# Threshold attention and a GELU MLP on one core: new sizes for the MLP portions of each slot, the fifth pair of heads turned by VectorE, x^T behind the next scores, and p regrouped in halves

## The chip, the cores and the metric

The kernel runs on one core of one Trainium2 chip. The metric is the time of one execution on the device in microseconds (us). Each kernel is run several times, and every run of the kernel before that is quoted beside it was made on the same chip. Two chips were used: the runs on the tail copies, gelus at once, regrouping whole and the loads were made on one, the other eight runs of the experiments on the other, so a comparison between those two groups, of traces too, crosses chips. A kernel on one core has no second core to compare its clock with, so single runs are compared through medians and 95% intervals.

Engines are named as the profile names them: PE is TensorE (PEld its weight loads), DVE is VectorE, ACT is ScalarE, POOL is GpSimd, SP is SyncE.

## The reference

Attention for 8 batches of 8 heads, 576 rows and 64 columns. In each row only the scores within tau = 0.02 of the row's maximum are kept. The 8 heads of a row, side by side, are the input x of an MLP with an exact GELU. All is float32, but the MLP's weights arrive as float64 and must be converted on the chip.

```python
def _attn_ref(q, k, v, tau):
    scale = 1.0 / np.sqrt(q.shape[-1])
    scores = scale * np.matmul(q, k.transpose(0, 1, 3, 2))
    thresh = np.max(scores, axis=-1, keepdims=True) - tau
    scores = np.where(scores >= thresh, scores, -1000000000.0)
    scores = scores - np.max(scores, axis=-1, keepdims=True)
    attn = np.exp(scores)
    attn = attn / (np.sum(attn, axis=-1, keepdims=True) + 1e-09)
    return np.matmul(attn, v).astype(np.float32)

def _moe_ref(x, w_in, w_out):          # x: 4608 x 512, w_in: 512 x 2048
    h = x @ w_in
    g = 0.5 * h * (1.0 + erf(h / sqrt(2)))
    return (g @ w_out).astype(np.float32)
```

## The kernel before

Two heads make a pair; there are 32 pairs of 5 chunks (four of 128 query rows and a tail of 64 rows of each head), hence 160 **slots**. In each slot PE makes the scores of one chunk, DVE takes the row maximum, ACT the exp, DVE masks and sums (this frees the score banks in PSUM), then p is transposed ("turned"), and the MLP of tokens that are ready fills PE's spare time. The first 20 slots take chunks 0 and 1 of the first four pairs, then their other chunks.

There are two ways of turning. For *early* pairs PE transposes q, k and p by products with the identity or with a diagonal that also scales. For *late* pairs DVE transposes blocks of 32 x 32 into `pd`, and DMA regroups those into `pT`. Then x^T = v^T p^T is a product on PE.

```python
    EARLY = HP + 1                  # HP = 4: five pairs are turned by PE

    def turn_p(p, i):               # a late pair, chunk i, by VectorE
        ...
        for e in reversed(range(n)):
            to = pd_tail[p % 2] if i == NC else pd[e][:, :, i * Q:(i + 1) * Q]
            nc.vector.transpose(to[:, 0:NB, :], w[:, e * S:(e + 1) * S].rearrange("p (b i) -> p b i", i=Q))
        if i == NC - 1:             # all four main chunks are there: regroup them in eight transfers
            s["pT"] = [one.tile([P, KR, S], FP32, tag=f"pT{e}", name=f"pT{e}") for e in range(2)]
            for e in range(2):
                for a in range(4):
                    regroup(s["pT"][e], a * P, P, pd[e], a)
        ...
    def block_steps(n):             # the MLP of one block of 256 tokens
        ...                         # hT: 4 products with w_in for each j
            if j % 2:
                t = gp.tile([P, 2, TOK], FP32, tag="g", name="g")
                nc.scalar.activation(t, hT, AF.Gelu)
        ...                         # o_ps: products with w_out

    PART = (1.0, 1.2, 1.0, 1.0, 0.8)          # share of MLP work in each slot of a pair
    for n in range(len(slots) + WEIGH + 1):   # [cut] the loop over slots
        scores(p, i)
        softmax_head(p, i)                    # maximum, exp
        owed += (goal(n) - goal(n - 1)) * BLK_NS * (PART[i] if not early and p < NP else 1.0)
        if early and n % 2:
            fill(owed, tokens)                # MLP, in every other early slot
        if last and last[0] < EARLY:
            turn_p_early(*last)               # PE turns the slot before
        softmax_tail(p, i, early)             # mask, sum, scale
        if not early and i:
            for c in range(0 if i == 1 else i, i + 1):
                turn_p(p, c)
        ...
        convert(3000 if n < 2 * HP else 3400) # float64 weights to float32, on VectorE
        ...                                   # x^T of early pairs
        if not early:
            fill(owed, tokens)
        if p > EARLY and i == WEIGH:          # x^T of the pair before, at the end of its slot
            for h in range(2):
                weigh_v(p - 1, h * HALF, (h + 1) * HALF)
```

## Time and profile before

| | before |
|---|---|
| median of 3 runs | 1493.13 us (1492.93 to 1494.76) |
| the profiled run | 1498.07 us, span 1496.3 us |
| granted PE clock, mean | 0.988 |
| PE / DVE / ACT busy | 97% / 61% / 43% of the span |

### The profile page before, as it was taken

What the parts mean: (1) busy time and instruction counts of PE and PEld (TensorE: products, weight loads), DVE (VectorE), ACT (ScalarE), POOL (GpSimd) and SP (SyncE); (2) the same over time, 40 slices, a digit from 0 to 9 for tenths busy, and PEclk for the clock granted to TensorE, in tenths of its full rate; (3) what the DMA queues carried; (4) which work ended last, traced back from release to release, by engine and by line L of the source; (5) the groups of instructions that cost most, each with busy time, mean ns of one, the idle gap of its engine ahead of it and who ended that gap; (6) DMA issues with size and microseconds to landing.
All of it is one profiled execution on the core that took longest, in us unless ns stands there. A gap on an engine that the chain in (4) does not pass through costs nothing.

```text
span 1496.3 us, 17938 instructions
## 1 busy us (share of the span) xinstructions
PE 1451.5 (97%) x6388; PEld 921.7 (62%) x6388; DVE 908.4 (61%) x2083; ACT 644.2 (43%) x952; POOL 40.5 (3%) x86
## 2 busy tenths in 40 slices
PE   7889898999999999999999999999999999999998
PEld 5567565547475756565666656565656575765764
DVE  6887748787767777777767766776676676000000
ACT  5566545736464545444444435363535252110110
POOL 3122000000000000000000000000000000000000
PEclk9899999999999999999999999999999999999999
DMA  9867313556555555554545455555554433200000
GB/s 281 251 217 237 80 32 80 112 118 120 107 109 104 107 107 102 104 104 96 104 83 106 97 117 104 117 103 111 98 109 94 98 73 70 57 15 11 4 14 14
DMA packets 381448, 152.12 MB, mean 102 GB/s; under 512 B 225456, under 2 KB 370608, under 8 KB 381360
## 3 DMA queue, kind: packets, MB, share of 16 engines
q1 hardware_dynamic: 371792, 116.84, 39.0%
q0 software_dynamic: 7168, 33.54, 6.6%
q8 instruction: 52, 0.85, 0.2%
q10 hardware_dynamic: 2400, 0.59, 0.2%
q14 instruction: 36, 0.29, 0.1%
HBM read 61.85 MB, written 9.44 MB: 48 GB/s over the span
## 4 chain that ended last, share of the span: by engine, by line
PE 87%; DVE 6%; DMA 3%; ACT 2%; SPq 2%; issue 1%; DVEq 0%; ACTq 0%
PE o_ps L454 32%; PE hT L443 32%; PE sc L339 11%; PE xT L415 10%; DVE p L364 2%; SPq L404 2%; DVE nmx L350 2%; PE tr L285 1%; DVE pd L392 1%; DMA q<-in_q_dram 1%; DMA k<-in_k_dram 1%; ACT p L351 0%; DMA pT<-pd 0%; ACT L351 0%; DVE power L176 0%
## 5 line engine op out<-in xcount | busy, mean ns | idle before, releaser
L443 PE MATMUL hT<-x,w_in 128*128 128x256 f32 x2304 | 524.2, 385 | 0.0
L454 PE MATMUL o_ps<-w_out,g 128*128 128x512 f32 x1152 | 515.4, 598 | 0.0
L443 PEld LDWEIGHTS hT<-x,w_in 128*128 128x128 f32 x2304 | 437.1, 192 | 88.3 <-issue 28.1
L454 PEld LDWEIGHTS o_ps<-w_out,g 128*128 128x128 f32 x1152 | 214.8, 190 | 259.3 <-issue 256.1
L350 DVE TENSOR_REDUCE nmx<-sc 128x1 f32<-128x576 f32 x288 | 205.7, 751 | 250.1 <-PE sc L339 249.8
L351 ACT ACTIVATE p<-sc,nmx 128x576 f32<-128x576 f32 x288 | 202.5, 740 | 302.5 <-DVE nmx L350 302.1
L364 DVE SCALAR_TENSOR_TENSOR p<-sc,thr,p 128x576 f32<-128x576 f32 x288 | 225.3, 816 | 56.8 <-ACT p L351 44.8
L415 PE MATMUL xT<-pT,v 128*64 128x288 f32 (+2 forms) x1280 | 171.0, 418 | 11.1 <-issue 4.7
L339 PE MATMUL sc<-kT,qT 64*128 64x288 f32 x960 | 160.0, 437 | 9.5 <-DVE p L364 9.1
L392 DVE STREAM_TRANSPOSE pd<-p 128x576 f32<-128x576 f32 x216 | 151.7, 750 | 5.8 <-DMA pT<-pd 5.2
L415 PEld LDWEIGHTS xT<-pT,v 128*64 128x64 f32 x1280 | 93.7, 140 | 85.6 <-issue 20.9
L339 PEld LDWEIGHTS sc<-kT,qT 64*128 64x128 f32 x960 | 88.6, 189 | 84.7 <-issue 65.0
L447 ACT ACTIVATE g<-hT 128x512 f32<-128x512 f32 x144 | 85.3, 597 | 124.7 <-PE hT L443 123.8
L380 DVE TENSOR_SCALAR p<-p,rden 128x576 f32<-128x576 f32 x215 | 104.6, 518 | 4.7
L351 ACT ACT_TABLE_LOAD x78 | 100.1, 1283 | 13.4 <-DVE nmx L350 12.2
L447 ACT ACT_TABLE_LOAD x79 | 101.4, 1283 | 9.4 <-PE hT L443 8.0
L424 ACT COPY x<-xT 128x256 f32<-128x256 f32 (+7 forms) x124 | 28.8, 285 | 145.9 <-PE xT L415 145.9
L457 ACT COPY o_sb<-o_ps 128x512 f32<-128x512 f32 x36 | 21.0, 583 | 150.2 <-PE o_ps L454 147.0
L285 PE MATMUL tr<-diag,p 128*128 128x128 f32 (+1 forms) x450 | 57.2, 290 | 0.0
L285 PEld LDWEIGHTS tr<-diag,p 128*128 128x128 f32 (+1 forms) x450 | 50.2, 187 | 11.2 <-issue 4.1
L378 ACT ACTIVATE p<-p,rden 128x576 f32<-128x576 f32 x28 | 21.7, 776 | 42.7 <-DVE rden L369 42.7
L339 PE MATMUL sc<-kT,q_tail 128*128 128x288 f32 x120 | 34.5, 410 | 5.5 <-DVE p L364 5.4
(69 smaller groups left out, 466.8 us busy)
## 6 DMA issues: line engine op xcount, KB each, us to landing
pT<-pd SPq DMA_DIRECT2D x216, 320.0 KB, 5.9
out_dram<-o_sb SPq DMA_DIRECT2D x36, 256.0 KB, 2.4
pT<-pd_tail SPq DMA_DIRECT2D x108, 80.0 KB, 3.2
q<-in_q_dram SPq DMA_DIRECT2D x108, 72.0 KB, 2.6
k<-in_k_dram SPq DMA_DIRECT2D x108, 72.0 KB, 2.9
v<-in_v_dram SPq DMA_DIRECT2D x162, 40.0 KB, 2.2
raw<-in_moe_w_in_dram POOLq DMA_DIRECT2D x8, 512.0 KB, 8.5
pd<-in_moe_w_in_dram POOLq DMA_DIRECT2D x8, 512.0 KB, 5.9
```

The costliest lines, as they stand in the source:

```text
L285: nc.tensor.matmul(to, lhsT=w[:, cols], rhs=diag[:, e, :], start=True, stop=True)
L339: nc.tensor.matmul(sc[e][:, h, 0:HALF], lhsT=lhsT, rhs=s["kT"][rows, at:at + HALF], start=True, stop=True)
L350: nc.vector.tensor_reduce(nmx[:, e:e + 1], sc, axis=AXIS.XY, op=ALU.max, negate=True)
L351: nc.scalar.activation(w[:, e * S:(e + 1) * S].rearrange("p (h s) -> p h s", h=2), sc, AF.Exp, bias=nmx[:, e:e + 1], scale=1.0)
L364: nc.vector.scalar_tensor_tensor(row, sc[e][:, :, 0:HALF], thr[:, e:e + 1], row, op0=ALU.is_ge, op1=ALU.mult, accum_out=den[:, e:e + 1])
L380: nc.vector.tensor_scalar(row, row, rden[:, e:e + 1], None, op0=ALU.mult)
L392: nc.vector.transpose(to[:, 0:NB, :], w[:, e * S:(e + 1) * S].rearrange("p (b i) -> p b i", i=Q))
L404: nc.sync.dma_start(to[:, :, at:at + n], src[a * Q:(a + 1) * Q])
L415: nc.tensor.matmul(xT[f, 0:hi - lo], lhsT=s["v"][:, e, c, :], rhs=pT[:, c, lo:hi], start=(c == 0), stop=(c == KR - 1))
L443: nc.tensor.matmul(hT[:, j % 2, :], lhsT=w_in_sb[c][:, j * P:(j + 1) * P], rhs=x_blk[n][:, c, :], start=(c == 0), stop=(c == N_DM - 1))
L447: nc.scalar.activation(t, hT, AF.Gelu)
L454: nc.tensor.matmul(o[:, 0:d_model], lhsT=g[j][:, m * P:(m + 1) * P], rhs=w_out_sb[j], start=(j == 0), stop=(j == N_DF - 1))
```

## The change

It has these parts. (1) MLP portions of late slots are fitted to each slot's room up to slot 42, and are nearly even from there. (2) The fifth pair is turned by VectorE, no longer by PE. (3) x^T stands directly behind the next scores instead of at a slot's end. (4) p is turned in every slot and regrouped in two halves, so that the transfers start earlier. (5) Gelus are held back by up to two, so that the next slot's exps go first, and a small exp brings its table back ahead of need. (6) Early slots have an MLP portion each, and the tail chunk's transposes come after the mask. (7) Some copies of the q and k tails go from VectorE to ScalarE, and some of the scalings of p in the other direction. (8) Later loads of q, k and v are issued from GpSimd.

```diff
-    EARLY = HP + 1
+    EARLY = HP
@@ load(p)
+        eng = nc.sync if p < HP + 2 else nc.gpsimd
-                    nc.sync.dma_start(t[e * D + f:e * D + f + Q], rows[:, :, f:f + Q])
+                    eng.dma_start(t[e * D + f:e * D + f + Q], rows[:, :, f:f + Q])
@@ turn_qk_early: tails of q and k
-        nc.vector.tensor_copy(kT[:, S:S + TAIL], tr[:, 1, 0:TAIL])
+        nc.scalar.copy(kT[:, S:S + TAIL], tr[:, 1, 0:TAIL])
[two more of this kind cut]
@@ softmax_tail
-            if e == 0 and n == 2 and p < 3 * HP:
+            if e == 0 and n == 2 and shared:      # ScalarE scales
@@ regroup(p, i), called at i = 2 (as 1), 3 and 4
+            half = slice((i - 1) * Q, (i + 1) * Q)
+            for e in (1, 0):
+                nc.sync.dma_start(s["pT"][e][:, :, a * P:(a + 1) * P][:, :, half], pd[e][rows, :, half])
@@ the MLP
+    def gelus(left):
+        while len(late) > left:
+            g, j, hT = late.pop(0)
+            ...
+            nc.scalar.activation(t, hT, AF.Gelu)
+    def table():                                  # a tiny exp brings the exp table back
+        if dirty[0]:
+            nc.scalar.activation(warm[:, 1:2], warm[:, 0:1], AF.Exp)
-                nc.scalar.activation(t, hT, AF.Gelu)
+                late.append((g, j, hT))
+                gelus(lag[0])
@@ the loop over slots
-    PART = (1.0, 1.2, 1.0, 1.0, 0.8)
+    PARTS = (1.36, 1.36, 0.5, 1.36, 0.42), (1.1, 1.1, 0.5, 1.2, 1.1)
+        if not early or n % 2 == 0:
+            gelus(0)
+            table()
+        for args in due:                          # x^T of early pairs, one slot later
+            weigh_v(*args)
+        if p > EARLY and i == WEIGH:              # x^T of late pairs, behind the scores
+            for h in range(2):
+                weigh_v(p - 1, h * HALF, (h + 1) * HALF)
-        if early and n % 2:
+        if early:
             fill(owed, tokens)
-        if last and last[0] < EARLY:
+        if last and last[0] < EARLY and last[1] < NC:
             turn_p_early(*last)
-            softmax_tail(p, i, early)
-            if not early and i:
-                for c in range(0 if i == 1 else i, i + 1):
-                    turn_p(p, c)
+            softmax_tail(p, i, early, batch == 1 and not busy)
+            if not early:
+                turn_p(p, i)
+                if i == 2:
+                    regroup(p, 1)
+                if i > 2:
+                    regroup(p, i)
+        if last and last[0] < EARLY and last[1] == NC:
+            turn_p_early(*last)
+            lag[0] = 2 if p < NP else 0
[cut: the last weight pieces leave pd; loads of the fifth pair; when tokens become ready]
```

More of the change, by code (lines that the diff above doesn't have):

```diff
@@ L138, in load_piece @@
         k = loaded[0] - 1
-        if k % 2:
+        if k % 2 and k < len(pieces) - 4:
             room = pd[k // 2 % 2][:, 0:NB - 2, :].bitcast(U32).rearrange("p b i -> p (b i)")
@@ L216, in load @@
                 n = min(KR, NB - r * KR)
-                nc.sync.dma_start(t[r:P:4, e, 0:n, :], rows[:, r * KR:r * KR + n, :])
+                eng.dma_start(t[r:P:4, e, 0:n, :], rows[:, r * KR:r * KR + n, :])
     def load_early(p):
@@ L267, in turn_qk_early @@
             nc.tensor.transpose(tr[:, j, 0:TAIL], s.pop(name)[0:TAIL, NC, :], ident[0:TAIL, 0:TAIL])
-        nc.vector.tensor_copy(kT[:, S:S + TAIL], tr[:, 1, 0:TAIL])
-        nc.vector.tensor_copy(kT[D:P, 0:TAIL], tr[D:P, 1, 0:TAIL])
+        nc.scalar.copy(kT[:, S:S + TAIL], tr[:, 1, 0:TAIL])
+        nc.scalar.copy(kT[D:P, 0:TAIL], tr[D:P, 1, 0:TAIL])
         for e in range(2):
             rows = slice(e * D, (e + 1) * D)
-            nc.vector.tensor_scalar(
-                qt[rows, e * TAIL:(e + 1) * TAIL], tr[rows, 0, 0:TAIL], q_scale[rows], None, op0=ALU.mult)
+            nc.scalar.activation(
+                qt[rows, e * TAIL:(e + 1) * TAIL], tr[rows, 0, 0:TAIL], AF.Copy, bias=0.0, scale=q_scale[rows])
     def turn_p_early(p, i):
@@ L354, in softmax_head, with softmax_tail @@
         nc.vector.tensor_scalar(thr[:, 0:n], nmx[:, 0:n], -1.0, tau_eff, op0=ALU.mult, op1=ALU.subtract)
-    def softmax_tail(p, i, early):
+    def softmax_tail(p, i, early, shared):
         s = st[p]
@@ L392, in turn_p, with regroup @@
             nc.vector.transpose(to[:, 0:NB, :], w[:, e * S:(e + 1) * S].rearrange("p (b i) -> p b i", i=Q))
-        if i == NC - 1:
+    def regroup(p, i):
+        s = st[p]
+        if i == 1:
             s["pT"] = [one.tile([P, KR, S], FP32, tag=f"pT{e}", name=f"pT{e}") for e in range(2)]
-            for e in range(2):
-                for a in range(4):
-                    regroup(s["pT"][e], a * P, P, pd[e], a)
-        if i == NC:
-            for a in range(4):
-                e, at = divmod(a * Q, TAIL)
-                regroup(s["pT"][e], MAIN + at, Q, pd_tail[p % 2], a)
-    def regroup(to, at, n, src, a):
-        nc.sync.dma_start(to[:, :, at:at + n], src[a * Q:(a + 1) * Q])
+        for a in range(4):
+            rows = slice(a * Q, (a + 1) * Q)
+            if i == NC:
+                e, at = divmod(a * Q, TAIL)
+                nc.sync.dma_start(s["pT"][e][:, :, MAIN + at:MAIN + at + Q], pd_tail[p % 2][rows])
+                continue
+            half = slice((i - 1) * Q, (i + 1) * Q)
+            for e in (1, 0):
+                nc.sync.dma_start(s["pT"][e][:, :, a * P:(a + 1) * P][:, :, half], pd[e][rows, :, half])
     def weigh_v(p, lo, hi):
@@ L431 @@
     BLK_NS = N_DF * (N_DM * NS_IN + TOK // P * NS_OUT)
+    late = []
+    lag = [1]
+    dirty = [False]
+    warm = const.tile([P, 2], FP32, name="warm")
+    nc.vector.memset(warm, 0.0)
+    def gelus(left):
+        while len(late) > left:
+            g, j, hT = late.pop(0)
+            t = gp.tile([P, 2, TOK], FP32, tag="g", name="g")
+            nc.scalar.activation(t, hT, AF.Gelu)
+            g[j - 1], g[j] = t[:, 0, :], t[:, 1, :]
+            dirty[0] = True
+    def table():
+        if dirty[0]:
+            nc.scalar.activation(warm[:, 1:2], warm[:, 0:1], AF.Exp)
+            dirty[0] = False
     def block_steps(n):
-        g = []
+        g = {}
         for j in range(N_DF):
@@ L445, in block_steps @@
             if j % 2:
-                t = gp.tile([P, 2, TOK], FP32, tag="g", name="g")
-                nc.scalar.activation(t, hT, AF.Gelu)
-                g += [t[:, 0, :], t[:, 1, :]]
+                late.append((g, j, hT))
+                gelus(lag[0])
         for m in range(TOK // P):
@@ L451, in block_steps @@
                 yield NS_OUT, len(pieces) - N_DF + j + 1
+                if j not in g:
+                    gelus(0)
                 if j == 0:
@@ L495 @@
     WEIGH = 2
-    START = 2 * HP + 1
+    START = 2 * HP + 2
     GOAL = [(-1, 0.0), (START - 1, 0.0), (BATCH - 1, 0.55)]
@@ L505, in goal @@
         return GOAL[-1][1]
-    PART = (1.0, 1.2, 1.0, 1.0, 0.8)
+    PARTS = (1.36, 1.36, 0.5, 1.36, 0.42), (1.1, 1.1, 0.5, 1.2, 1.1)
     tokens = 0
     owed = 0.0
+    due = []
     for n in range(len(slots) + WEIGH + 1):
@@ L519 @@
             softmax_head(p, i)
-        owed += (goal(n) - goal(n - 1)) * BLK_NS * (PART[i] if not early and p < NP else 1.0)
-        if early and n % 2:
+        busy = len(late)
+        if not early or n % 2 == 0:
+            gelus(0)
+            table()
+        for args in due:
+            weigh_v(*args)
+        due = []
+        if p > EARLY and i == WEIGH:
+            for h in range(2):
+                weigh_v(p - 1, h * HALF, (h + 1) * HALF)
+        owed += (goal(n) - goal(n - 1)) * BLK_NS * (PARTS[n > 2 * BATCH + WEIGH][i] if not early and p < NP else 1.0)
+        if early:
             fill(owed, tokens)
             owed = 0.0
-        if last and last[0] < EARLY:
+            table()
+        if last and last[0] < EARLY and last[1] < NC:
             turn_p_early(*last)
         if p < NP:
-            softmax_tail(p, i, early)
-            if not early and i:
-                for c in range(0 if i == 1 else i, i + 1):
-                    turn_p(p, c)
+            softmax_tail(p, i, early, batch == 1 and not busy)
[7 more added lines that the diff above has]
+            turn_p_early(*last)
         if p < HP - 1 and i == 0:
@@ L539 @@
         if p < HP and i == NC and 0 < p < HP - 1:
-            if p + 3 < EARLY:
-                load_early(p + 3)
-                load_v_early(p + 3)
-            else:
-                load(p + 3)
+            load(p + 3)
         if n == BATCH:
@@ L550 @@
         if p >= HP - 1 and i == 2 and p + 1 < NP:
-            (turn_qk if p + 1 >= EARLY else turn_qk_early)(p + 1)
+            turn_qk(p + 1)
         convert(3000 if n < 2 * HP else 3400)
-        if last and last[0] < EARLY:
-            done, hp = divmod(last[0], HP)
-            if last[1] == 1:
-                weigh_v(last[0], 0, TOK)
-                if hp == HP - 1:
-                    tokens = done * S + TOK
-            if last[1] == NC:
-                weigh_v(last[0], TOK, S)
-                if hp == HP - 1:
-                    tokens = (done + 1) * S
         if not early:
+            lag[0] = 2 if p < NP else 0
             fill(owed, tokens)
             owed = 0.0
-        if p > EARLY and i == WEIGH:
-            for h in range(2):
-                weigh_v(p - 1, h * HALF, (h + 1) * HALF)
-            if p % HP == 0:
-                tokens = p // HP * S
-    convert(1e12)
+        if last and last[0] < EARLY:
+            if last[1] == 1:
+                due.append((last[0], 0, TOK))
+            if last[1] == NC:
+                due.append((last[0], TOK, S))
+        if n == START - 1:
+            tokens = TOK
+        elif n == BATCH + 1:
+            tokens = S
+        elif p > EARLY and i == WEIGH and p % HP == 0:
+            tokens = p // HP * S
     fill(1e12, B * S)
```

## The prediction

> **What bounds the kernel now.** I read the page first: TensorE (PE) is busy 97% of a 1496.3 us span, and the chain that ended last is 87% PE. Busy time does not say whether PE runs at its pace, so I then asked for busy time by stretch and for PE's waits. Columns of the first fence: stretch, its length, then busy us (and instructions) of PE, PEld, VectorE (DVE), ScalarE (ACT), POOL, the granted clock, the DMA share, GB/s. In the second: who waited for whom, total us, times, longest, for the first 220 us.
>
> ```profile
> 11.40:88.50 77.10, 63.91 (x393) 45.81 (x393) 67.30 (x163) 46.53 (x93) 15.81 (x29) 0.91 0.83 257
> 88.50:174.40 85.90, 77.32 (x430) 57.56 (x429) 65.33 (x161) 55.70 (x95) 15.10 (x31) 0.94 0.68 206
> 174.40:333.70 159.30, 148.07 (x652) 87.26 (x654) 112.25 (x263) 78.88 (x120) 0.62 (x2) 0.97 0.39 78
> ...
> 400.00:1255.00 855.00, 855.00 (x3754) 530.69 (x3754) 604.97 (x1364) 390.54 (x535) 0.00 (x0) 1.00 0.51 102
> ```
> ```profile
> PE sc L339 <- DVE p L364: 7.7, 8, 2.3
> PE tr L259 <- DMA q<-in_q_dram: 6.5, 1, 6.5
> PE xT L415 <- issue: 4.7, 2, 2.6
> PE xT L415 <- DVE pT L296: 3.6, 4, 2.5
> ```
>
> The reader is to see that from 400 us on PE never stops, at full clock, while DVE has 250 us to spare in 855. Starts of successive hT records there are 216 ns apart, of o_ps records 429 ns, with about 0.09 us more at each change of kind; nothing but PE work can be taken out of that part. All loss that can be recovered lies before about 330 us: PE idles, the clock falls to 0.91, and DVE (67.3 of 77.1 us in the first stretch) is nearly the limit. I count slots (one chunk of scores, softmax and turning) by their score groups (sc, L339): slot 20 starts at 171.3 us, slot 26 at 223.2, slot 42 at 327.1. From slot 42 on the MLP work left is the same in both programs, so **the question is when slot 42 starts**.
>
> Four lines of the merged timeline (start, duration, instruction, idle before) show the costliest habit of the early part:
>
> ```profile
> 97.85 1.42 PE L285 MATMUL tr<-diag,p 128*128 128x128 f32 x10
> 98.94 0.76 DVE L296 COPY pT<-tr 128x256 f32<-128x256 f32 x2 [3.18 <-PE tr L285]
> ...
> 99.51 3.15 PE L415 MATMUL xT<-pT,v 128*64 128x320 f32 x20 [0.25 <-DVE pT L296]
> ...
> 100.08 0.82 DVE L364 SCALAR_TENSOR_TENSOR p<-sc,thr,p 128x576 f32<-128x576 f32 x1
> ```
>
> VectorE stands 3.18 us for a transpose that PE put behind 5.9 us of MLP, and only then masks p, which releases the score banks.
>
> **What the Trainium skill says.** (1) "ScalarE: Activation LUTs", What ACT_TABLE_LOAD costs: 1283 ns for the load and about 1380 ns of drain. The trace agrees on the load (157 of mean 1283 ns) but shows no drain: an exp ends at 96.27, the load starts at 96.29 and the next ACTIVATE at 97.58. (2) "TensorE: Matmul & The Clock Gate", Part 1: after idle windows of 3.4 us the clock is halved. The trace agrees: halved stretches of 3.41 or 6.83 us, eight of them (34.1 us in all) between 24 and 291 us, then none until the last 3 us. (3) "Perfetto Trace Analysis", Summary: the profiler window per engine type: on the software path an issue lasts until its descriptors are written. Before, POOL's issues of 128 rows take 0.533 us, so at most 4.2 ns a row. (4) "SBUF — State Buffer", SBUF: two separate sides: VectorE's two-port operations keep GpSimd from writing descriptors. No run here shows it yet; the change moves 26 pairs of loads there.
>
> **The change part by part.** I compared the two programs' order of instructions, and costed it with durations from the trace.
>
> *Fifth pair by VectorE.* PE loses 55 transposes (3219 matmuls become 3164), of two records at 112 ns: 12.3 us. DVE gains nine transposes of p (0.72 each), five to nine scalings (0.52) and 1.7 for q and k.
>
> *Slots 0 to 9.* The q/k tails (1.05 us of DVE a pair: 0.22 + 0.23 + 0.58) go to ScalarE, with their waits for PE (1.84 and 0.95). DVE is the pace here, three of them fall inside: 3 x 1.05 + about 2 of waits, **-5**.
>
> *Slots 10 to 19.* MLP portions come in each slot (3.0 us) instead of every other (5.6), the tail's transposes come after the mask, and x^T comes behind the next scores. I walked the slots with two rules: scores start when PE is done and the last mask has ended; DVE starts when the scores (1.25 us) and its own work are done. Full slot: 3.75 us to rden, plus 3.55 of weight conversion; tail slots 2.9 + 3.55; slots 11, 14, 17 carry 1.2 of tail copies and about 1.2 of waiting for PE; slot 17 also turns the fifth pair's q and k. In slots 12, 15 and 18 PE has 1.17 scores + 3.2 x^T + 3.0 MLP + 2.25 transposes, and needs banks that ScalarE frees only after two exps, a table load, a gelu, another load and the copies: about 11 to 13 us each. The last weight pieces no longer lie in pd; one takes block 0's x tile and waits for its hT in slot 18: about 3 us. The walk gives 86 us, and before has 85.9: **0**.
>
> *Slots 20 to 25.* Before 174.4 to 224.5 (DVE starts), 50 us. After: the pair as below 31, slot 25 some 6, conversions and tail copies left over 4.5: 41.5, **-8.6**.
>
> *Slots 26 to 41.* The portions 1.36, 1.36, 0.5, 1.36, 0.42 give PE 5.9, 5.9, 7.9, 5.9, 2 us a slot, plus 0.25 for changes of kind. DVE per full slot, from the timeline of slot 28 (reduce at 231.41, rden done 235.16, turned 237.2): 5.75, or 6.3 where it scales both halves; 1.73 more in slot 2, 4.25 in the tail slot. Neither exceeds the other by much; the walk gives 31 us a pair. Before, these 16 slots took 103.9 us (6.5 a slot, with PE waiting 9.6 for masks after 220 us and DVE 12 for exps between 175 and 345, behind table loads); after 16/5 x 31 = 99: **-5**.
>
> *From slot 42.* PE per slot goes from 4.9 ... 12.1 us to 7.1 ... 8.7, sum unchanged. Both are PE-bound, so evening it gains only the last gaps before 400 us (1.3 + some small ones: -2). Gelus now stand behind the next slot's exps and hold banks longer. Reading which bank each accumulation takes, only slots 87, 142 and 152 have an x^T that needs a gelu of the same slot early: ready at 1.25 + 2.25 + 1.28 + 0.60 = 5.4 us after the scores' start, wanted at 3.7: 3 x 1.8 = **+5**. Together +3.
>
> *Regrouping in halves.* 256 B packets take 18 ns (median, from 14,976 such), those of 512 B 27 (up to 80 under load): 36 for 27 at worst, and the DMA share of 0.51 stays far from full. Issues: 640 packets x 18 / 16 engines = 0.72 us, about 14 us a pair instead of 12. The tail lands some 3 us ahead of its x^T in slots 26 to 41. Nothing on the path.
>
> *Loads from GpSimd.* Estimate: 576 rows x 4.2 ns = 2.4 us, eight of them and eight of 0.5: 23 us a pair, under the 31 to 37 available, asked for six slots (about 40 us) ahead.
>
> Sum: -5 + 0 - 8.6 - 5 + 3 = -15.6; 1493.1 - 15.6 = 1477.5, say **1478 us**. PE's 12.3 us aren't added: they lie in slots 20 to 25, counted there.
>
> **Rivals.** (a) *The early walk is too gloomy*: if the heavy slots 12, 15, 18 overlap better, slots 0 to 19 give 15 more, as the DVE sum of 133 us in 163 allows; 1463. For it: conversions can be caught up. Against: ScalarE's two table loads stand ahead of the copies that free PE's banks. (b) *A new wait for gelu*: four mm banks, two held late; if exps come later than I think, x^T and hT waits recur at most hT slots, about 25 x 1 us: 1500. For it: a slot has only about 1 us between DVE's work and PE's. Against: before, DVE waits 208 us for scores after 345, so exps are prompt. (c) *GpSimd becomes the bound*: at 10 ns a row, 48 us a pair, against 37: +250 us. For it: VectorE's scalings may lock it out. Against: 0.533 us for 128 rows. (d) *Transfers*: hidden anyway, 0.
>
> **Range and chances.** (a) sets the low end, 1464; (b) in half, with a smaller gain early, sets 1490. Faster by 2% needs below 1463.3, that is twice the gain: 0.14. Slower by 2% needs (c): 0.03. Same: 0.83.
>
> **What would show each step.** Slot 42's scores start near 309 us (a gain of 18); slot 20's near 166; the stretch from slot 20 to 26 has 41 us. PE transposes of p: 360 records for 450. Table loads fall well below 157. After 400 us PE is busy throughout except a few waits of x^T or hT for g, about 5 us. POOL's issues of q and k last under 3 us. I am wrong if slot 42 starts before 297 or after 320, if PE idles over 15 us after 400, or if DVE waits for q and k landing.

## More of the kernel before

The line of totals on the page of the kernel before gives each engine's busy time, its share of the span and its instructions.

```profile
PE 1451.5 (97%) x6388; PEld 921.7 (62%) x6388; DVE 908.4 (61%) x2083; ACT 644.2 (43%) x952; POOL 40.5 (3%) x86
```

Four groups from the costliest groups of the same page follow: line, engine, operation, output and input, shapes and count, then busy time and mean ns of one, and idle time before them with what ended it.

```profile
L380 DVE TENSOR_SCALAR p<-p,rden 128x576 f32<-128x576 f32 x215 | 104.6, 518 | 4.7
L351 ACT ACT_TABLE_LOAD x78 | 100.1, 1283 | 13.4 <-DVE nmx L350 12.2
L447 ACT ACT_TABLE_LOAD x79 | 101.4, 1283 | 9.4 <-PE hT L443 8.0
L285 PE MATMUL tr<-diag,p 128*128 128x128 f32 (+1 forms) x450 | 57.2, 290 | 0.0
```

The reader is to see three things that the change touches: the scaling of p, which costs 518 ns on DVE; the table loads on ACT, half of which stand at the exp (L351) and half at the gelu (L447); and 450 transposes of p on PE.

Busy time by stretch, between the first maximum of slots 20, 26 and 42 (columns: stretch, length, then busy us and instructions of PE, PEld, DVE, ACT, POOL, granted clock, DMA share, GB/s):

```profile
174.40:224.50 50.10, 47.44 (x241) 28.02 (x241) 25.84 (x69) 18.87 (x41) 0.62 (x2) 1.00 0.12 24
224.50:333.70 109.20, 100.63 (x412) 59.23 (x414) 86.41 (x195) 60.01 (x79) 0.00 (x0) 0.95 0.52 103
```

In slots 20 to 25 PE is the limit (47.44 of 50.10) and DVE has half of the time free. In slots 26 to 41 both have gaps, and the clock is not always whole.

## The result, and the profile after

The changed kernel is correct. Its median is 1477.28 us of 4 runs (1474.17 to 1478.69), against 1493.03 us for the kernel before (4 runs, 1490.19 to 1494.76). The ratio is 0.9894, with a 95% interval of 0.9872 to 0.9916: about 1% faster, and within the 2% that count as the same. A ratio is the mean time of one kernel's fast runs over that of the other's of the same rounds, so it is not quite the ratio of the medians quoted.

One caution for all comparisons of traces: the profiled run of before is its slowest (1498.07 us), that of after its fastest (1474.17 us). The two traces differ by 23.9 us, the medians by 15.7.

Totals and groups of the page of the changed kernel, to be put beside those of before:

```profile
PE 1429.3 (97%) x6288; PEld 904.8 (61%) x6288; DVE 931.8 (63%) x2098; ACT 642.6 (44%) x1014; POOL 294.3 (20%) x502
...
L381 DVE TENSOR_SCALAR p<-p,rden 128x576 f32<-128x576 f32 x240 | 120.2, 536 | 4.9
...
L448 ACT ACT_TABLE_LOAD x81 | 103.9, 1283 | 1.4
L455 ACT ACT_TABLE_LOAD x80 | 102.6, 1283 | 1.4
...
L286 PE MATMUL tr<-diag,p 128*128 128x128 f32 (+1 forms) x360 | 47.9, 296 | 8.5 <-ACT g L448 4.6
```

The transposes of p are 360 for 450, as predicted. The table loads at the exp and the gelu are 161 for 157, which was not: holding gelus back moved the second load of each couple from the exp (L351) to the small exp (L455) and made none of them go away. The scaling lasts 536 ns for 518 (see the run on the loads).

Busy time by stretch of the changed kernel, same columns as before. The stretches end at the first maximum of slots 10, 20, 26 and 42; the last lies far behind:

```profile
11.20:81.00 69.80, 58.10 (x376) 42.47 (x376) 63.66 (x150) 49.36 (x105) 15.32 (x28) 0.90 0.93 283
81.00:165.10 84.10, 75.57 (x427) 55.69 (x426) 67.17 (x160) 60.52 (x104) 20.14 (x38) 0.94 0.66 205
...
400.00:1240.00 840.00, 835.16 (x3658) 518.25 (x3657) 597.61 (x1333) 382.22 (x573) 177.05 (x291) 1.00 0.58 100
```

```profile
165.10:206.10 41.00, 36.95 (x125) 16.94 (x126) 35.69 (x81) 15.82 (x24) 16.21 (x29) 0.96 0.58 111
206.10:303.00 96.90, 93.24 (x432) 56.12 (x434) 88.66 (x197) 49.70 (x77) 28.59 (x48) 1.00 0.76 127
```

Slots 20 to 25 shrank from 50.10 to 41.00 us. PE lost 10.5 us of work there, and DVE, 25.84 us before, now has 35.69: it idles 5.3 us there and PE 4.1 (at a clock of 0.96). Slots 26 to 41 have PE busy 93.24 of 96.90 us at the full clock. After 400 us PE stood still for 4.8 of 840 us, where it had not stood still before. The waits of PE in that part of the changed kernel (who waits for whom, total us, times, longest) are one line:

```profile
PE xT L419 <- ACT g L448: 4.8, 3, 1.6
```

These are the three x^T products that need a bank which a held-back gelu frees; they come at 655.8, 1101.6 and 1184.2 us, in slots 87, 142 and 152, the three that the prediction read out of the order of banks.

PE's waits of the changed kernel in the first 220 us, and four lines of its timeline (start, length, instruction, idle before) at the place where the prediction showed the costly habit:

```profile
PE sc L340 <- DVE p L365: 12.5, 6, 4.9
PE tr L260 <- DMA q<-in_q_dram: 8.0, 2, 6.2
PE tr L286 <- ACT g L448: 4.6, 3, 2.7
PE tr L286 <- ACT pT L294: 2.3, 3, 0.8
```

```profile
88.44 0.82 DVE L365 SCALAR_TENSOR_TENSOR p<-sc,thr,p 128x576 f32<-128x576 f32 x1
...
89.10 1.42 PE L286 MATMUL tr<-diag,p 128*128 128x128 f32 x10
...
90.33 0.73 DVE L297 COPY pT<-tr 128x256 f32<-128x256 f32 x2
90.44 1.24 PE L340 MATMUL sc<-kT,qT 64*128 64x288 f32 x8
```

The mask now comes first and DVE reaches the transposes as they are done; the next scores start 0.1 us later. In exchange, PE waits more for masks (12.5 us for 7.7). It no longer waits for VectorE's copies of p^T (3.6 us before), but for ScalarE instead: 4.6 us for gelus and 2.3 us for ScalarE's copies of p^T.

The table sets the steps side by side. Slots are counted by their first scores record; the end of a stretch is the start of the next.

| stretch | before | after | change in the two traces | predicted |
|---|---|---|---|---|
| to slot 20 | 171.3 | 163.8 | -7.5 | -5 |
| slots 20 to 25 | 51.9 | 41.0 | -10.9 | -8.6 |
| slots 26 to 41 | 103.9 | 96.6 | -7.3 | -5 |
| slot 42 to the end | 1169.2 | 1171.0 | +1.8 | +3 |
| span | 1496.3 | 1472.4 | -23.9 | -15.6 |

How far is one trace to be trusted? Seven of the kernels below have the instructions of the changed one up to slot 20. In these eight traces the first maximum of slot 10 comes at 81.0 to 82.5 us, and that of slot 20 at 163.5 to 166.3. The first scores of slot 42 came at 301.4 us in the changed kernel and at 305.9 us in a kernel that is the same up to there. From slot 42 on, variants of the changed kernel with the same instructions agree to 0.1 us. So the 8 us by which the two traces differ beyond the medians most likely lie before slot 42 (of the kernel before there is one trace only), and each position there is good to some 2 to 5 us.

Much of this scatter is the granted clock, and so is part of the gain. In the traces the clock is either whole or, for 3.41 or 6.83 us at a time, one half, and then successive hT records start 427 ns apart for 216. From the first maximum of slot 26 to that of slot 42, five kernels with the changed order (with either portions) have no half clock and take 95.8 to 97.8 us, with PE idle for 1.1 to 3.7 us; two others have 3.4 us of it and take 98.6 us, one of them (one gelu left before x^T) with the same ScalarE order there as the changed kernel. The kernel before has 10.2 us of it there, in a stretch of 109.2 us with PE idle for 8.6. If PE does half its work at half the clock, about 5 of the 12.2 us that this stretch lost from before to after (109.2 to 96.9) are clock; this is an estimate. More waiting of PE and more half clock come together in these traces; which brings on which was not tested.

### The profile page after: what moved, and what is told of

The parts are those of the page before. It is cut to its first block, busy times and chain, and to the rows that moved or that the text cites. A ratio compares the mean times of both kernels' runs of the same rounds, so it can differ in the third digit from the quotient of the medians.

```text
span 1472.4 us, 18592 instructions
## 1 busy us (share of the span) xinstructions
PE 1429.3 (97%) x6288; PEld 904.8 (61%) x6288; DVE 931.8 (63%) x2098; ACT 642.6 (44%) x1014; POOL 294.3 (20%) x502
## 4 chain that ended last, share of the span: by engine, by line
PE 85%; DVE 7%; ACT 4%; DMA 2%; SPq 2%; issue 1%; DVEq 0%; ACTq 0%
PE o_ps L480 33%; PE hT L468 31%; PE sc L340 11%; PE xT L419 9%; DVE nmx L351 2%; DVE p L365 1%; DMA q<-in_q_dram 1%; ACT p L352 1%; ACT L448 1%; SPq L228 1%; DVE power L176 1%; PE tr L286 1%; DVE pd L393 1%; ACT L455 1%; DMA pT<-pd 0%
## 5 line engine op out<-in xcount | busy, mean ns | idle before, releaser
L468 PE MATMUL hT<-x,w_in 128*128 128x256 f32 x2304 | 518.7, 382 | 0.0
L351 DVE TENSOR_REDUCE nmx<-sc 128x1 f32<-128x576 f32 x288 | 205.7, 751 | 234.3 <-PE sc L340 234.1
L210 POOL DMA_DIRECT2D q<-in_q_dram x104 | 70.0, 679 | 647.5 <-DVE q_tail L328 401.9
L419 PE MATMUL xT<-pT,v 128*64 128x288 f32 (+2 forms) x1280 | 165.2, 411 | 4.8 <-ACT g L448 4.8
L393 DVE STREAM_TRANSPOSE pd<-p 128x576 f32<-128x576 f32 x224 | 160.4, 754 | 1.7 <-ACT p L379 1.3
L381 DVE TENSOR_SCALAR p<-p,rden 128x576 f32<-128x576 f32 x240 | 120.2, 536 | 4.9
L218 POOL DMA_DIRECT2D v<-in_v_dram x208 | 111.1, 536 | 60.4 <-DMA k<-in_k_dram 35.4
L448 ACT ACT_TABLE_LOAD x81 | 103.9, 1283 | 1.4
L455 ACT ACT_TABLE_LOAD x80 | 102.6, 1283 | 1.4
L210 POOL DMA_DIRECT2D k<-in_k_dram x104 | 72.7, 705 | 0.0
L286 PE MATMUL tr<-diag,p 128*128 128x128 f32 (+1 forms) x360 | 47.9, 296 | 8.5 <-ACT g L448 4.6
L286 PEld LDWEIGHTS tr<-diag,p 128*128 128x128 f32 (+1 forms) x360 | 40.7, 190 | 17.7 <-ACT g L448 6.0
```

The costliest lines, as they stand in the source:

```text
L210: eng.dma_start(t[e * D + f:e * D + f + Q], rows[:, :, f:f + Q])
L351: nc.vector.tensor_reduce(nmx[:, e:e + 1], sc, axis=AXIS.XY, op=ALU.max, negate=True)
L381: nc.vector.tensor_scalar(row, row, rden[:, e:e + 1], None, op0=ALU.mult)
L419: nc.tensor.matmul(xT[f, 0:hi - lo], lhsT=s["v"][:, e, c, :], rhs=pT[:, c, lo:hi], start=(c == 0), stop=(c == KR - 1))
L455: nc.scalar.activation(warm[:, 1:2], warm[:, 0:1], AF.Exp)
L468: nc.tensor.matmul(hT[:, j % 2, :], lhsT=w_in_sb[c][:, j * P:(j + 1) * P], rhs=x_blk[n][:, c, :], start=(c == 0), stop=(c == N_DM - 1))
```

## The experiments

All twelve kernels were correct. Unless it is said otherwise, each is the changed kernel with one edit and was timed in 5 rounds against the kernel before. "Against the changed kernel" is the difference of the two ratios times 1493 us; both intervals are about 3 us wide to either side, so a difference under some 4 us is not settled by the times alone.

| run | median us | ratio to before (95%) | against the changed kernel | scores of slot 42 | slot 42 to end |
|---|---|---|---|---|---|
| changed | 1477.28 | 0.9894 (0.9872 to 0.9916) | | 301.4 | 1171.0 |
| fifth pair back on PE | 1478.24 | 0.9902 (0.9884 to 0.9920) | +1.2 | 306.0 | 1171.1 |
| tail copies back on VectorE | 1479.79 | 0.9910 (0.9891 to 0.9930) | +2.4 | 305.7 | 1171.0 |
| old portions up to 42 | 1475.53 | 0.9885 (0.9865 to 0.9905) | -1.3 | 296.2 | 1176.9 |
| gelus at once | 1475.21 | 0.9874 (0.9849 to 0.9898) | -3.0 | 308.3 | 1165.1 |
| regrouping whole | 1514.75 | 1.0146 (1.0120 to 1.0172) | +37.6 | 334.3 | 1177.4 |
| loads from SyncE | 1473.75 | 0.9869 (0.9845 to 0.9893) | -3.7 | 301.5 | 1171.0 |
| one gelu left before x^T | 1470.37 | 0.9848 (0.9827 to 0.9869) | -6.9 | 305.9 | 1165.1 |
| scaling half on ScalarE | 1481.73 | 0.9920 (0.9903 to 0.9938) | +3.9 | 306.2 | 1171.0 |
| early order as before | 1482.00 | 0.9916 (0.9899 to 0.9934) | +3.3 | 308.8 | 1171.0 |
| late pairs as before | 1480.10 | 0.9908 (0.9886 to 0.9931) | +2.1 | 309.8 | 1167.7 |
| three edits together | 1465.36 | 0.9805 (0.9783 to 0.9827) | -13.3 | 294.4 | 1167.1 |
| before, fifth pair alone | 1491.26 | 0.9971 (0.9950 to 0.9993) | +11.5 | 321.5 | 1170.5 |

### The fifth pair: one part undone, and one part alone

Undone in the changed kernel:

```diff
-    EARLY = HP
+    EARLY = HP + 1
@@ and its loads and its q, k turned as those of an early pair
```

> The changed kernel with the fifth pair turned by TensorE again (55 transposes more on PE, slots 20 to 24 with the early order). Theory (the walk by slots): slots 20 to 25 took 41.0 us between DVE starts, they go back towards the 50.1 of before, so 6 to 10 us later from slot 26 on to the end: about 1485 us. Rival (the gain of this stretch came from the new order of x^T and tails, not from who turns the pair): at most 3 us, about 1479.

The median was 1478.24 us: the theory, 1485, fell, and the rival held. Slots 20 to 25 took 44.80 us for 41.00, and the busy times of this run say why it is so little:

```profile
162.60:207.40 44.80, 44.80 (x234) 26.48 (x234) 27.68 (x71) 21.75 (x43) 17.56 (x31) 1.00 0.18 46
```

PE is busy all 44.80 us and DVE 27.68. In the changed kernel PE has 36.95 and DVE 35.69 of 41.00. Moving the pair takes 7.9 us off PE and puts 8.0 us on DVE; it buys 3.8 us in this stretch. DVE is then nearly as busy as PE, each waits for the other, and the changed kernel has one 3.41 us window of half clock there where this run has none. With the pair on PE the stretch still took 5.3 us less than the 50.10 of before; that much is not due to who turns the pair. Slot 20 came 2.5 us earlier in this run than in the changed kernel and 0.9 us earlier than in any of the eight traces; the loads of the fifth pair differ before it.

Alone, as an edit of the kernel before (with the last weight pieces taken out of `pd`, which the pair needs):

```diff
-    EARLY = HP + 1
+    EARLY = HP
-        if k % 2:
+        if k % 2 and k < len(pieces) - 4:
```

> The kernel before with one part of the change alone: the fifth pair turned by VectorE (with the last weight pieces out of the room that it needs). Theory of the prediction (nearly the whole gain of slots 20 to 25 is PE's loss of these 55 transposes, 8.6 us): slots 20 to 26 take 42 us for 50, the end 1484 to 1486 us. Rival, from the run that gave the fifth pair back to TensorE (it costs 1 to 4 us): 20 to 26 take 47 to 50 us, the end 1489 to 1493 us.

Both were half right. Slots 20 to 25 fell by 11.3 us, more than the theory's 8, but the end only moved by 4.3 us (ratio 0.9971), as the rival said. The two stretches of this run, from slot 20 to 26 and to 42:

```profile
176.10:214.90 38.80, 32.58 (x110) 15.26 (x110) 33.24 (x79) 13.04 (x20) 0.42 (x1) 1.00 0.19 41
214.90:329.50 114.60, 105.40 (x462) 61.80 (x463) 86.36 (x195) 60.78 (x83) 0.00 (x0) 0.99 0.62 122
```

PE lost 14.9 us in the first stretch. Of these, 10.9 are the transposes; the rest is mostly x^T: the trace has 20 records of it there for 60 before, and 145 for 96 in the next stretch, where PE's busy time rose by 4.8 us and the length by 5.4. A late pair's x^T stands in the third slot of the next pair, so part of the gain was only moved across slot 26. This shift belongs to the changed kernel too (20 records, then 124).

### The early order

```diff
-        for args in due: weigh_v(*args)       # x^T at the end of the same slot again
-        if early:
+        if early and n % 2:
             fill(owed, tokens)
-        if last and last[0] < EARLY and last[1] < NC:
+        if last and last[0] < EARLY:          # the tail's transposes ahead of the mask again
             turn_p_early(*last)
[cut: tokens become ready for the MLP one slot earlier again]
```

> The changed kernel with the order of the early slots as before: MLP portions only in odd slots, the tail chunk's transposes ahead of the mask, x^T at the end of the same slot. The fifth pair stays with VectorE and the tail copies with ScalarE. Theory (this order is what takes 4 to 8 us off slots 0 to 20): slot 20 (first reduce) at 169 to 173 us for 165, the end at 1481 to 1485 us. Rival (VectorE sets the pace of slots 0 to 20 and the order does nothing): slot 20 within 163 to 167 us, the end within 2 us of 1477.

The theory held at slot 20: its first maximum came at 173.4 us, where the eight traces with the same instructions as the changed kernel have 163.5 to 166.3. The wait that the prediction had pointed at is back in this run, up to slot 20:

```profile
DVE pT L297 <- PE tr L286: 7.3, 2, 4.2
```

The changed kernel has 0.7 us of it, the kernel before 7.6. The end moved +3.3 us by ratio, +4.7 by medians, which is less than slot 20 did. In the two traces themselves nothing is given back: this run is 7.4 us behind at the first scores of slots 20 and 42 and at the end (308.8 for 301.4, spans 1479.8 and 1472.4). The difference is that the trace of the changed kernel is of its fastest run, 3.1 us under its median.

### The tail copies

```diff
-        nc.scalar.copy(kT[:, S:S + TAIL], tr[:, 1, 0:TAIL])
+        nc.vector.tensor_copy(kT[:, S:S + TAIL], tr[:, 1, 0:TAIL])      # and two more of this kind
```

> The changed kernel with the q and k tails copied by VectorE again (four pairs, 1.05 us each, with their waits for PE). Theory (VectorE is the pace in slots 0 to 9): slot 10 starts 4 to 6 us later and the end too, about 1482. Rival (the early part waits for transfers and for PE, so the copies are hidden): within 2 us, about 1478.

+2.4 us by ratio, and slot 10 at 83.1 us, 0.6 to 2.1 later than in the eight traces with the changed copies. This lies between theory and rival and inside the intervals; a small gain is likely and not shown.

### The portions up to slot 42

```diff
-    PARTS = (1.36, 1.36, 0.5, 1.36, 0.42), (1.1, 1.1, 0.5, 1.2, 1.1)
+    PARTS = (1.0, 1.2, 1.0, 1.0, 0.8), (1.1, 1.1, 0.5, 1.2, 1.1)
```

> The changed kernel with the old portions 1.0, 1.2, 1.0, 1.0, 0.8 up to slot 42 alone. Theory: fitted portions are what lets VectorE run on between slots 26 and 41, so 3 to 5 of the 7.3 us gained there are lost, plus one more x^T that waits for a gelu (four instead of three, 1.9 us): about 1483. Rival (the gain there is that exp no longer waits for a table load): within 1 us of the changed kernel apart from that extra wait, about 1479.

The theory fell: 1475.53 us, no slower. Slot 42's scores came at 296.2 us. Some 2 us of that is MLP work left for later (slots 42 to 62 take 157.1 us for 155.1); the rest of what it gained came back as waits, which we put down to another order of accumulations that takes other banks (argued, not tested):

```profile
PE xT L419 <- ACT g L448: 8.1, 5, 1.6
```

Five waits for three. So the fitted portions up to slot 42 had no part in the gain that these runs can show.

### Gelus at once, and one gelu fewer held back

```diff
-                gelus(lag[0])
+                gelus(0)
```

> The changed kernel with each gelu issued as soon as its hT is done, none held back. Theory: from slot 42 on PE is the bound, late exps cost nothing there and the three waits of x^T for gelu (5.7 us) go; between slots 20 and 42 exps wait 1.3 us for their table in hT slots, some 9 x 1 us; so within 4 us of the changed kernel, 1473 to 1481. Rival (holding gelus back is what keeps VectorE on pace everywhere): over 10 us slower, above 1487.

1475.21 us. (One gelu was held back in early slots too; this edit ends that as well.) Slot 42 came 2 to 7 us later than in the two traces of the changed order (301.4 and 305.9), and from there to the end took 1165.1 us for 1171.0, with no wait of PE after 400 us. The two sides cancel or slightly more: holding gelus back was worth nothing on the whole in the form it had. The number of table loads is 161 here as well, 69 of them at the exp again.

The waits come from slots with an x^T, so it is enough to hold back less there:

```diff
-            lag[0] = 2 if p < NP else 0
+            lag[0] = (1 if i == 1 and n > 2 * BATCH else 2) if p < NP else 0
```

> The changed kernel, from slot 41 on holding one gelu instead of two back in the slot before x^T. By the banks this takes away all three waits of x^T for a gelu (5.7 us in the trace). Theory: 5 to 6 us faster, about 1472. Rival: the gelu's table load then stands ahead of the next slot's exps, VectorE gets 1.3 us late there and PE waits for it instead: 0, about 1477.

1470.37 us, and 1165.1 us from slot 42 to the end: 5.9 us less, and no wait of PE after 400 us. The theory held. ScalarE's instructions are in the order of the changed kernel until slot 87, and the two traces keep a constant distance except at slots 87, 142 and 152, where the changed kernel falls back by 1.9, 2.0 and 2.1 us: the three waits cost more than the 4.8 us listed. By ratio this kernel is 3.9 us under the one with gelus at once, so holding back may be worth that much where it holds no bank that x^T needs; this is at the edge of what the times settle, and the two were run on different chips.

### Who scales p in slots 20 to 41

```diff
-            softmax_tail(p, i, early, batch == 1 and not busy)
+            softmax_tail(p, i, early, batch == 1)
```

> The changed kernel with ScalarE scaling one half of p in every slot of batch 1, also where gelus wait. Theory (VectorE is the pace between slots 20 and 42: 124 of 138 us busy): it loses 0.52 us in each of some nine hT slots, so 3 to 5 us faster, about 1473. Rival (ScalarE has two table loads and two gelus in these slots, so its scaling comes late and VectorE waits for it): 0 to 4 us slower, about 1479.

Slower, as the rival had it: 1481.73 us. Slots 26 to 41 took 103.1 us where the changed order takes 95.8 to 98.6. In this stretch PE waits 6.4 us for masks, four times, where the changed kernel has 3.7 us, three times. The rest of the difference is PE's busy time, 96.75 us for 93.24, at a granted clock of 0.97 for 1.00. The wait that the rival named is there too; from the first maximum of slot 20 to that of slot 42 this run has

```profile
DVE pd L393 <- ACT p L379: 6.7, 5, 1.9
```

VectorE stands for ScalarE's scaling 6.7 us, and in the changed kernel 1.3 us. The rule "scale on ScalarE only when no gelu is pending" is worth about 4 us by ratio, at the edge of what the times settle; the stretch shows it more clearly.

### The late pairs: regrouping, and the whole package

Regrouping whole, with x^T still behind the scores:

```diff
-        if i == 1:
+        if i == NC - 1:
             s["pT"] = [...]
-                nc.sync.dma_start(s["pT"][e][:, :, a * P:(a + 1) * P][:, :, half], pd[e][rows, :, half])
+                nc.sync.dma_start(s["pT"][e][:, :, a * P:(a + 1) * P], pd[e][rows])
-                if i == 2:
-                    regroup(p, 1)
```

> The changed kernel with each main regrouping in one piece of 320 KB at slot 3, eight transfers instead of sixteen. Theory: the half of slots 0 and 1 then leaves pd two slots later, so VectorE's turning in slot 0 of the next pair waits for it, 3 to 5 us a pair where VectorE is the pace (four pairs), less than 1 us where PE is: 10 to 20 us slower, about 1490. Rival (transfers are hidden anyway): 0, 1477.

1514.75 us, 37.6 us slower, and more than the theory's 10 to 20. DVE's and PE's waits of this run (the whole execution for DVE, up to 340 us for PE):

```profile
DVE pd L393 <- DMA pT<-pd: 67.0, 35, 7.9
...
DVE pd L393 <- DMA pT<-pd_tail: 13.3, 8, 2.6
```

```profile
PE sc L340 <- DVE p L365: 35.1, 15, 6.8
```

DVE may not overwrite `pd` with chunk 0 of the next pair before the regrouping has read it. In the kernel before, chunk 0 was turned only in slot 1, which gave the transfer a slot more. In the changed kernel it is turned in slot 0, so the transfer must have started earlier, and the halves do that.

The whole package undone: whole regrouping, chunks 0 and 1 turned together in slot 1, and x^T at the end of slot 2.

```diff
 [the edit above, and]
-        if p > EARLY and i == WEIGH: ...      # from behind the scores
+        if p > EARLY and i == WEIGH: ...      # to the end of the slot, after fill
-                turn_p(p, i)
+                for c in range(0 if i == 1 else i, i + 1 if i else 0):
+                    turn_p(p, c)
```

> The changed kernel with the late pairs arranged as before: whole regrouping after the fourth chunk, chunks 0 and 1 turned together in slot 1, x^T at the end of slot 2; all else as changed. Theory (what gains between slots 26 and 42 is this package, since neither the portions nor the scaling account for it): 26 to 42 goes from 97 to 105 to 109 us, and the end is at 1478 to 1483 us even though the x^T waits for gelus after slot 42 go (about 5.7 us less there). Rival (the gain there is that of the held-back gelus, which let exps go first, and the package is only a shift of order): 26 to 42 stays within 97 to 100 us, and with slots 42 on 5.7 shorter the end is 1471 to 1474 us.

The theory held: slots 26 to 41 took 107.5 us (105 to 109 was expected) and the median is 1480.10 us.

```profile
206.60:314.10 107.50, 99.63 (x442) 58.92 (x444) 89.88 (x200) 49.56 (x77) 28.62 (x48) 0.97 0.57 121
```

Against the 96.90 us of the changed kernel PE is idle 7.9 us for 3.7, at a lower clock, while DVE has the same work to within 1.2 us. After slot 42 the run gains 3.3 us and not the 5.7 expected: x^T at the end of the slot still meets a held-back gelu, twice and for 1.9 us in all, for three times and 4.8 us. The package is thus worth 4 to 8 us before slot 42 and 2 us at the end, and the first of these the traces show, though half clock (0.97 for 1.00) is part of it; the second of which the times don't settle.

### The loads

```diff
-        eng = nc.sync if p < HP + 2 else nc.gpsimd
+        eng = nc.sync
```

> The changed kernel with the loads of q, k and v from pair 6 on issued by SyncE again. Theory: hidden either way, within 2 us, about 1477. Rival 1 (SyncE, with 20 regroupings a pair and everything in order, gets late and x^T or the turning of q and k waits): 1485 or more. Rival 2 (descriptor writing by GpSimd is slowed by VectorE or slows it): faster by 3 us or more, about 1473.

1473.75 us, a ratio 3.7 us below the changed kernel's; the intervals overlap, and slot 42's scores are at 301.5 us for 301.4. Issuing from GpSimd gained nothing that shows. It had a small cost on VectorE, which this line of the run from SyncE shows beside that of the changed kernel (536 ns):

```profile
L381 DVE TENSOR_SCALAR p<-p,rden 128x576 f32<-128x576 f32 x240 | 115.8, 518 | 4.9
```

In the changed kernel 25 of the 240 scalings took over 560 ns, up to 719; here none did. All 25 overlap an issue of GpSimd.

### The three edits that helped, together

Old portions up to slot 42, one gelu left before x^T, all loads from SyncE.

> The changed kernel with three of the earlier edits together: even portions up to slot 42 as well, one gelu (not two) left waiting before the x^T products of the late pairs, and all q, k, v loads issued from SyncE. Theory (each gain keeps, and the waits of x^T for gelus that the even portions brought back after slot 42 go): slot 42 near 297 us, slot 42 to the end 1165 to 1166 us, so 1462 to 1467 us, some 11 us below the changed kernel. Rival (the gain of the even portions and the loss after slot 42 are one thing, MLP work that is only moved across slot 42): slot 42 earlier by 5 but the rest longer by as much, 1470 us, no better than with one gelu left alone.

1465.36 us, ratio 0.9805 (0.9783 to 0.9827): faster than both kernels, by about 2% against before, which is neither clearly over nor under that mark. It lies in the theory's range of 1462 to 1467. From slot 42 to the end it took 1167.1 us, a little more than the 1165 to 1166 expected; 2.0 us of that are MLP work moved behind slot 42, so the rival holds for that part. It has 179 table loads, more than any kernel here and 18 more than the changed one, and is the fastest. Slots 20 to 25, 26 to 41 and the stretch after 400 us:

```profile
163.60:201.00 37.40, 34.22 (x123) 16.13 (x124) 35.12 (x80) 15.79 (x24) 0.31 (x1) 1.00 0.45 86
201.00:297.30 96.30, 95.23 (x439) 58.01 (x439) 88.14 (x202) 55.99 (x83) 0.00 (x0) 1.00 0.72 133
400.00:1230.00 830.00, 830.00 (x3635) 513.39 (x3634) 591.00 (x1329) 395.86 (x581) 0.00 (x0) 1.00 0.54 101
```

PE is busy all of the last stretch and 95.23 of 96.30 us in slots 26 to 41. What is left to gain lies before slot 20, where PE still idles about 20 of 152 us and runs at 0.88 and 0.98 of its clock.

## Why the prediction was right or wrong

The predicted time, 1478 us, was right (1477.28), and so was its frame: all gain lies before slot 42, and behind it the kernel loses a little. That the sum fits to a microsecond is partly luck: two of its terms have the right size for reasons that failed, and the two traces differ by 23.9 us where the medians differ by 15.7.

- **What bounds the kernel.** Right. After 400 us PE is busy 835 of 840 us, and the edits of gelus and portions moved that part through PE's waits and PE's work alone.
- **Slots 0 to 19, predicted -5, the traces -7.5.** Right in size, wrong in cause. By first maximum nearly all of it lies before slot 10 (88.5 to 81.0 us); slots 10 to 19 took 84.1 us for 85.9, and 81.9 to 84.1 in the eight traces, where the walk gave 86. The failing step is the term for slots 0 to 9: it gave five us to the tail copies alone. Undoing these brings slot 10 back by 0.6 to 2.1 us; undoing the new order brings it back by 2.5 to 4.0 us (85.0), and slot 20 by 7 to 10. Up to slot 9, where neither order has had an MLP portion or a tail chunk, only the place of x^T differs, and it is worth 2.1 to 3.6 us there (77.6 us without it, 74.0 to 75.5 in the eight traces). The walk through slots 10 to 19 ("0") was 2 to 4 us too long, so rival (a), "the early walk is too gloomy", came true in small part.
- **Slots 20 to 25, predicted -8.6, the traces -10.9 by first scores and -9.1 by first maximum.** Right for the stretch. Wrong as a gain of the fifth pair: alone it takes 11.3 us off this stretch, but 5.4 return in the next with the x^T that moved, and 4.3 reach the end. Given back to PE inside the changed kernel it costs 1.2 us, which the times don't tell from nothing. The prediction compared stretches and did not ask which work had crossed slot 26.
- **Slots 26 to 41, predicted -5, the traces -7.3.** Right in size, wrong in the reason. The fitted portions, whose sizes the walk was built on, did nothing for the time. The stretch grows from 96.9 us to 107.5 without the package of turning each slot, halves and early x^T, to 103.9 with gelus at once and to 103.1 with the scaling on ScalarE. In all three PE waits more and the clock is 0.97; the prediction's walk had no term for the clock. "Regrouping in halves ... nothing on the path" failed: without the halves the changed kernel is 37.6 us slower. They are no gain over the kernel before, but what the new order of turning stands on. The walk asked when pT would be ready and not when `pd` would be free.
- **From slot 42, predicted +3 of which +5 waits for gelu, measured +1.8.** Right to the slot: 87, 142 and 152. The waits cost 5.9 us, as the edit that removes them shows, so the rest of this part gained 4.1 us where the prediction had 2.
- **Table loads "well below 157".** Wrong: 161. Batching gelus does not save loads if a slot still has an exp and a gelu in turn; it only chooses where they stand.
- **Loads from GpSimd.** Right that they do no great harm: issues of q and k took 0.68 and 0.70 us, eight in a pair, against an estimate of 2.4. Rival (c) was far off.
- **Rival (b)**, new waits at most hT slots: didn't come; PE has only three such waits after 400 us, and three of 4.6 us in the first 220.

Do the parts make up the 15.7 us? Undoing them one by one costs 1.2 (fifth pair), 2.4 (tails), 3.3 (early order), 2.1 (late package) and 3.9 (scaling), and gains 1.3 (portions), 3.0 (gelus) and 3.7 (loads). That sums to a cost of 4.9, so the parts do not add: each stands in for others, as the fifth pair shows, which is worth 4.3 us alone and 1.2 beside the rest. With errors of some 4 us each no finer account can be given.

## What to carry to other kernels

When work moves from the engine that sets the pace to another, look in the same stretch at how busy the other one is: 8 us moved to an engine that then had as little to spare bought 4 us, and part of what a stretch gains may only have crossed its end. Holding work back that frees a buffer is paid for where somebody needs that buffer; reading which bank each accumulation takes found the three waits in advance, and holding one less at those places removed them. Compare waits in the stretch that differs and not over a longer window, where a gain elsewhere can hide a loss. A change made of many parts may hold several that do nothing or harm: here undoing three parts in full or in places brought 1465 us for 1477.

## What the Trainium skill lacked or had wrong

- "ScalarE: Activation LUTs", What ACT_TABLE_LOAD costs, has 1283 ns for the load and about 1380 ns of drain. The load is 1283 ns in every trace; the drain was not seen: in the trace of before an exp ends at 96.27 us, the load starts at 96.29, and the next ACTIVATE at 97.58.
- "SBUF — State Buffer", SBUF: two separate sides, calls the port pair of VectorE and GpSimd an exclusive lock and warns that VectorE keeps GpSimd from writing descriptors. Of the other direction it says that VectorE then blocks, and gives no time for VectorE behind an issue of GpSimd. With the loads issued from GpSimd the scaling of p (128 x 576) took 536 ns on average for 518 without, 25 of 240 over 560 and at most 719. These 25 began 0.2 to 0.3 us into an issue; 47 others overlapped an issue too and took at most 542 ns.
- "DMA: Bandwidth & Descriptors", Why small descriptors are slow (HBM only), says that transfers within SBUF don't suffer from small packets. The regrouping within SBUF took 27 ns a packet of 512 bytes in the median before, and 18 ns a packet of 256 bytes after; halving saves a third of a packet's time and not half, so the same bytes take 36 ns for 27. It was hidden here.
- "DMA: Bandwidth & Descriptors", Anatomy of one DMA — SWDGE (gpsimd) path, calls descriptor generation small and variable and gives no number by rows. Here an issue of 128 rows of weights took 0.54 us on GpSimd (median; the prediction's 0.533 is the shortest) and one of q or k, 576 rows of 128 bytes in the kernel, 0.68 to 0.70 us on average, for the 2.4 that the prediction estimated from 4.2 ns a row. Rows are not what the queue moves: the trace of the changed kernel has 16 packets of 4096 bytes and 16 of 512 for such an issue, where the run from SyncE has packets of 128 bytes, so no cost of a row follows from these runs.
